# A fused attention and gated-MLP kernel: norm jobs spread over two phases, output weights and splits in other slots

## The chip, the cores and the metric

The kernel runs on one core of a Trainium2 chip. The metric is the device time of one execution in microseconds. Five kinds of work can run beside each other: matrix products on TensorE (PE, with its weight loads PEld), elementwise work on VectorE (DVE), on ScalarE (ACT) and on GpSimd (POOL), and transfers between the chip's memory and its on-chip tiles. All transfers of this kernel are issued from the queue of SyncE (SP). Each engine and SP's queue take their instructions in program order: one that waits holds back all behind it.

## The reference

```python
# u, v: (4, 3008, 256); z: (4, 3008, 64), float32
scores = (z @ z.T) / S                      # S = 3008, for each of the 4 batches
attn = np.maximum(scores, 0.0) ** 2
x = u * (attn @ v)                          # (12032, 256)
rms = np.sqrt(np.mean(x * x, axis=-1, keepdims=True) + 1e-06)
xn = x / rms * rms_g
g = xn @ w_gate                             # w_gate, w_val: (256, 1536), float64
silu = g * (1.0 / (1.0 + np.exp(-g)))
out = (silu * (xn @ w_val)) @ w_out         # w_out: (1536, 256), float64
```

## The kernel before, in words

**Tiling.** The 3008 columns of a batch are cut into six chunks of 512 (the last has 448); two chunks make a *pair* `p`, so there are three pairs in a batch and twelve in all. All products are float32 products on PE, made of a high and a low part: a value is split into `hi` (rounded, made by ACT) and `lo` (the rest, made by DVE or POOL), and each product is three matmuls.

**Phases.** For each pair there is a phase A (attention) and a phase M (the MLP). They run in the order A0, A1, A2, M0, A3, M1, A4, M2 and so on: M lags by three pairs. Phase A has 24 steps, one for each block of 128 rows. A step makes the scores of step i + 2 (4 matmuls, lines 386 and 387, from `mh`, `ml` and `zst`), splits those of step i + 1 (ACT: relu at line 394, `H`; DVE: the square at line 401 and the low half `L` at line 426; in A0 to A2 half of the squares are made by ACT) and multiplies those of step i with `v` (12 matmuls, lines 465, 466 and 470). At its end `emit_gate` multiplies with `u` on DVE and stores `xg`. Where a score's transposed block is needed later, `emit_l` stores a copy (`kept`, from the tile `halves` in the ring `out`), and `load_turned` reads it back in place of a product.

Phase M has twelve *units* of 128 hidden columns. A unit does seven products with combined weights (A11, A12, S1, S2, S3, A22, S4: a Strassen-like scheme on 2 x 2 blocks; lines 664 to 666, from the splits `xh`, `xl` of the pair and the weights `wu`, read by `load_unit` two or three units ahead) and twelve matmuls with the output weights `woh`, `wol` (lines 692, 693 and 696).

**Jobs in slots.** All other work is cut into jobs that `at(phase, slot, fn)` puts into slots: 24 in an A phase (one a step), 36 in an M phase (three a unit). `hook` runs a slot's jobs where the phase's own code calls it, so a job stands in each engine's queue between the phase's own instructions. The jobs that matter here:

- *Norm of a pair* (`norm_jobs`, planned by `norm_plan`): 23 jobs, numbered 0 to 22. Jobs 0 to 7 square the two halves of `ux` on ACT and sum them on DVE, 8 is a small product on PE, 9 to 12 (`guess`, `cubic`, two `newton`) make the reciprocal root on 32 columns, 13 to 18 turn it back and scale `ux` (two transposes, four multiplications of 512 columns), 19 to 22 are four subtractions of 512 columns that make S1, S2, S3 and A22.
- *Splits of a pair* (`split_jobs`, `plan_splits`): seven values, for each a high half on ACT and, a slot later, a low half on DVE.
- *Weights' parts*: the float64 weights come as pairs of 32-bit words (tile `wraw`, in the ring `T` that `wu` and the read-back blocks share) and are decoded by five operations on DVE. `prep_wout(f)` makes the output weights of units f and f + 1 (two operations on ACT and eight pieces on POOL besides: lines 186 and 187). `prep_proj(j)` makes the projections' weights for four units: four parts, then nine `ends` in which `put` writes a high half (ACT), a low half (POOL, four pieces by `pool_pieces`) and two stores to `wcomb`.
- *Batch loads* (`plan_batch`): six chunks of `z` and twelve of `v` of the next batch, each a load, a high half on ACT and a low half on DVE (`z`) or POOL (`v`). Their loads go through a ring of six buffers (`new_raw("batch")`: `mh0`, `ml0`, `mh1`, `ml1` and two of `raw`), which turns by one with each load that is called.

**Order.** `Beside.put` plans M phases: each slot has room for 0.75 us on DVE, every third slot 1.35 on ACT; a job goes into the first slot from its due time on that has room, or, where none has, into the one with the most room left. In A phases the slots are written out by hand. A number `g` from 0 to 71 counts the steps of A0, A1 and A2 together (`at_step`).

## Time and profile before

| | us |
|---|---|
| median of three runs | 2084.29 |
| lowest and highest | 2083.55 and 2086.81 |
| the profiled execution | 2084.4 |
| its span, first to last instruction | 2082.6 |
| PE busy in it | 2030.4 (97%) |
| DVE busy | 1595.1 (77%) |
| ACT busy | 1447.3 (69%) |
| POOL busy | 210.0 (10%) |
| mean granted clock of TensorE | 0.992 |

The span is what the trace covers; the rest of the execution's time lies before the first and behind the last instruction. A granted clock of 1.00 is 2.4 GHz, 0.50 is 1.2 GHz. PE's share is high throughout, so what a change can win or lose lies in the stretches in which PE waits or runs at the lower clock. POOL works mostly in the first fifth of the span, where the weights are decoded; after that it works only for batch loads.

### The profile page before, as it was taken

How to read it: one execution, taken by the hardware profiler on the slowest of the kernel's cores; microseconds unless marked ns; L12 is line 12 of the kernel's file. 1: busy time of each engine (PE TensorE's matmuls, PEld its weight loads, DVE VectorE, ACT ScalarE, POOL GpSimd, SP SyncE). 2: the span in 40 equal slices, each digit the busy share in tenths (PEclk: the TensorE clock that was granted, in tenths of full speed). 3: DMA queues.
4: the chain of work that ended last, by engine and by line, in shares of the span. 5: the costliest groups of instructions: out<-in, count | busy, mean ns of one | idle time of the engine just before them, and what ended most of it. 6: DMA issues, size and time to landing. Idle time of an engine off the chain costs nothing.

```text
span 2082.6 us, 27214 instructions
## 1 busy us (share of the span) xinstructions
PE 2030.4 (97%) x8968; PEld 1680.4 (81%) x8968; DVE 1595.1 (77%) x2633; ACT 1447.3 (69%) x2601; POOL 210.0 (10%) x376
## 2 busy tenths in 40 slices
PE   8998997899999999999999999999999999999999
PEld 7786876688888888888887888788888888888887
DVE  7888886887777777787876776879777687677765
ACT  8887865696577575787577565669756857466665
POOL 0155634200000000500000000130000000000000
PEclk9999998999999999999999999999999999999999
DMA  3244374155456487426355549634645636734342
GB/s 108 79 131 149 109 255 155 72 186 185 129 134 210 135 173 225 162 102 217 135 149 151 183 130 202 214 113 159 206 132 126 207 126 167 193 124 163 124 145 90
DMA packets 320654, 320.50 MB, mean 154 GB/s; under 512 B 196736, under 2 KB 235776, under 8 KB 320512
## 3 DMA queue, kind: packets, MB, share of 16 engines
q1 hardware_dynamic: 320512, 318.77, 50.5%
q8 instruction: 70, 1.15, 0.2%
q14 instruction: 72, 0.59, 0.1%
HBM read 190.78 MB, written 81.79 MB: 131 GB/s over the span
## 4 chain that ended last, share of the span: by engine, by line
PE 75%; DVE 3%; ACT 2%; DMA 1%; issue 1%; SPq 0%; ACTq 0%; DVEq 0%
PE ps L664 9%; PE ps L665 9%; PE ps L666 9%; PE po L465 9%; PE po L466 9%; PE po L470 8%; PE py L692 5%; PE py L693 5%; PE py L696 5%; PE ps L387 3%; PE ps L386 3%; ACT hH L676 1%; DMA raw<-in_zT 1%; DMA out_T<-y 1%; ACT s L671 1%
## 5 line engine op out<-in xcount | busy, mean ns | idle before, releaser
L465 PE MATMUL po<-H,vh 128*128 128x512 f32 (+1 forms) x1152 | 448.3, 389 | 7.6 <-DVE H L430 4.5
L466 PE MATMUL po<-H,vl 128*128 128x512 f32 (+1 forms) x1152 | 445.0, 386 | 0.0
L671 ACT COPY s<-ps 128x512 f32<-128x512 f32 (+1 forms) x432 | 249.8, 578 | 235.5 <-PE ps L666 235.4
L664 PE MATMUL ps<-xh,wu 128*128 128x512 f32 (+1 forms) x1008 | 393.5, 390 | 15.9 <-DMA wu<-wc 11.4
L665 PE MATMUL ps<-xh,wu 128*128 128x512 f32 (+1 forms) x1008 | 389.9, 387 | 2.0 <-DMA wu<-wc 2.0
L666 PE MATMUL ps<-xl,wu 128*128 128x512 f32 (+1 forms) x1008 | 389.3, 386 | 0.0
L470 PE MATMUL po<-L,vh 128*128 128x512 f32 (+1 forms) x1104 | 337.0, 386 | 2.6 <-DVE L L426 2.3
L676 ACT CAST hH<-s 128x512 fp32r<-128x512 f32 (+1 forms) x288 | 176.7, 614 | 202.8 <-DVE s L758 199.2
L426 DVE TENSOR_TENSOR L<-r,H 128x512 fp32r<-128x512 f32 x368 | 255.4, 706 | 52.8 <-ACT H L423 29.6
L401 DVE TENSOR_TENSOR r<-ps,r 128x512 f32<-128x512 f32 x328 | 214.6, 681 | 101.1 <-ACT r L394 100.6
L394 ACT ACTIVATE r<-ps 128x512 f32<-128x512 f32 (+1 forms) x392 | 216.2, 599 | 105.1 <-PE ps L387 93.3
L681 DVE TENSOR_TENSOR hL<-s,hH 128x512 fp32r<-128x512 f32 (+1 forms) x288 | 200.2, 695 | 105.4 <-ACT hH L676 92.3
L465 PEld LDWEIGHTS po<-H,vh 128*128 128x128 f32 x1152 | 216.5, 188 | 59.1 <-DVE H L430 10.4
L466 PEld LDWEIGHTS po<-H,vl 128*128 128x128 f32 x1152 | 216.7, 188 | 40.6
L470 PEld LDWEIGHTS po<-L,vh 128*128 128x128 f32 x1104 | 206.7, 188 | 44.6 <-DVE L L426 5.8
L664 PEld LDWEIGHTS ps<-xh,wu 128*128 128x128 f32 x1008 | 189.6, 188 | 63.0 <-ACT s L671 13.0
L692 PE MATMUL py<-hH,woh 128*128 128x512 f32 (+1 forms) x576 | 223.0, 387 | 8.1 <-ACT hH L676 8.0
L693 PE MATMUL py<-hH,wol 128*128 128x512 f32 (+1 forms) x576 | 222.5, 386 | 0.0
L665 PEld LDWEIGHTS ps<-xh,wu 128*128 128x128 f32 x1008 | 189.8, 188 | 37.6 <-DMA wu<-wc 3.1
L666 PEld LDWEIGHTS ps<-xl,wu 128*128 128x128 f32 x1008 | 189.6, 188 | 36.2
L423 ACT CAST H<-r 128x512 fp32r<-128x512 f32 x328 | 202.7, 628 | 1.2 <-DVE r L401 1.2
L696 PE MATMUL py<-hL,woh 128*128 128x512 f32 (+1 forms) x576 | 175.8, 386 | 0.0
(82 smaller groups left out, 2807.3 us busy)
## 6 DMA issues: line engine op xcount, KB each, us to landing
wu<-wc SPq DMA_DIRECT2D x288, 448.0 KB, 4.0
kept<-halves SPq DMA_DIRECT2D x168, 256.0 KB, 2.0
raw<-in_v SPq DMA_DIRECT2D x44, 256.0 KB, 4.2
u<-in_uT SPq DMA_DIRECT2D x40, 256.0 KB, 4.4
xg<-u SPq DMA_DIRECT2D x40, 256.0 KB, 2.1
raw<-in_zT SPq DMA_DIRECT2D x38, 256.0 KB, 4.9
ux<-xg SPq DMA_DIRECT2D x16, 512.0 KB, 4.9
out_T<-y SPq DMA_DIRECT2D x32, 256.0 KB, 2.2
```

Of the source, the lines that this page charges most:

```text
L394: nc.scalar.activation(a[:, :n], ps[:, :n], AF.Relu)
L426: nc.vector.tensor_tensor(lo[:, :n], a[:, :n], f32(hi[:, :n]), op=ALU.subtract)
L465: nc.tensor.matmul(po[d][:, :n], wh[:, j, ds], hi[:, :n], start=(i == 0), stop=False)
L466: nc.tensor.matmul(po[d][:, :n], wl[:, j, ds], hi[:, :n], start=False, stop=(ends and lo is None))
L470: nc.tensor.matmul(po[d][:, :n], wh[:, j, ds], lo[:, :n], start=False, stop=ends)
L664: nc.tensor.matmul(ps[:, :n], wh[:, o, :], xh[:, :n], start=start, stop=False, skip_group_check=True)
L665: nc.tensor.matmul(ps[:, :n], wl[:, o, :], xh[:, :n], start=False, stop=False, skip_group_check=True)
L666: nc.tensor.matmul(ps[:, :n], wh[:, o, :], xl[:, :n], start=False, stop=stop, skip_group_check=True)
L671: nc.scalar.copy(s, ps[:, :self.n])
L692: nc.tensor.matmul(acc[h, d][:, :n], woh[:, f, ds], hi[:, :n], start=(f == 0), stop=False)
L693: nc.tensor.matmul(acc[h, d][:, :n], wol[:, f, ds], hi[:, :n], start=False, stop=False)
L696: nc.tensor.matmul(acc[h, d][:, :n], woh[:, f, ds], lo[:, :n], start=False, stop=(f == NF - 1))
```

## The change

The ten last norm jobs of pair 0 move from A1 to A2's slots 2 to 11, and its first thirteen stand one in a slot from slot 5 on. Of pair 1's norm the first thirteen stay in M0 (due from slot 3), the last ten go to A3's slots 1 to 10; its splits move from A3's slots 0 to 6 to its slots 16 to 22. Pair 0's splits keep their slots but take another order, with A11 and A12 last. The output weights f = 4 and f = 6 move from M0 to A2, f = 0 and f = 2 three steps earlier, f = 8 and f = 10 get slots 9 and 15 of M0. Batch loads that reuse a buffer are put one slot later. The stores of the weights' parts, and of the kept copies of batch 0, are put on a list that the next hook empties first. The parts' halves use three pairs of tiles that the splits use later (`xh2`, `xl2`, `xh3`, `xl3`, `xh6`, `xl6`) in place of the ring `out`, and the third projection's decoded parts use the tiles of the first. Pair 2's `x` is loaded at M1's start, and its norm is due from slot 4.

```diff
--- before.py
+++ after.py
@@ -98,7 +98,15 @@
     def at(phase, slot, fn):
         jobs[phase, slot].append(fn)
 
+    late = []
+
+    def flush_late():
+
+        while late:
+            late.pop(0)()
+
     def hook(phase, slot):
+        flush_late()
         turns = [t for t in [fn() for fn in jobs.pop((phase, slot), ())] if t]
         while turns:
             for t in list(turns):
@@ -188,6 +196,8 @@
 
         return load, ops + [("a", 0.61, 0, high), ("d", 0.0, 0, low)]
 
+    outs = [2, 3, 6]
+
     def prep_proj(j, pool, tags):
 
         js = slice(j * CH, (j + 1) * CH)
@@ -206,18 +216,23 @@
             parts.append((load, ops + [("d", 0.0, 0, total)]))
 
         def put(o, value):
-            def high():
-                hi = work.tile([P, CH], F32R, tag="out", name="wohi", bufs=3)
-                lo = work.tile([P, CH], F32R, tag="out", name="wolo", bufs=3)
+            def both():
+                outs.append(outs.pop(0))
+                hi = moving.tile([P, CH], F32R, tag=f"xh{outs[-1]}", name="wohi")
+                lo = moving.tile([P, CH], F32R, tag=f"xl{outs[-1]}", name="wolo")
                 x = value()
                 nc.scalar.copy(hi, x)
                 pool_pieces(lo, x, f32(hi), ALU.subtract)
-                for h, t in enumerate((hi, lo)):
-                    nc.sync.dma_start(
-                        out=wcomb[j][:, :, h, o, :].rearrange("f p c -> p f c"),
-                        in_=f32(t).rearrange("p (f c) -> p f c", c=P),
-                    )
-            return high
+
+                def store():
+                    for h, t in enumerate((hi, lo)):
+                        nc.sync.dma_start(
+                            out=wcomb[j][:, :, h, o, :].rearrange("f p c -> p f c"),
+                            in_=f32(t).rearrange("p (f c) -> p f c", c=P),
+                        )
+
+                late.append(store)
+            return both
 
         def combine(key, x, y, op, into=None):
             def go():
@@ -442,9 +457,11 @@
                 else:
                     nc.scalar.copy(halves[:m], split)
                 r0 = 2 * (kt % 4) * P
-                nc.sync.dma_start(
-                    out=kept[b, kc, c][r0:r0 + 2 * m, :].rearrange("(p h) q -> p h q", h=2), in_=halves[:m]
-                )
+                rows = kept[b, kc, c][r0:r0 + 2 * m, :].rearrange("(p h) q -> p h q", h=2)
+                if b == 0:
+                    late.append(lambda rows=rows, part=halves[:m]: nc.sync.dma_start(out=rows, in_=part))
+                else:
+                    nc.sync.dma_start(out=rows, in_=halves[:m])
 
     acc = {}
 
@@ -891,7 +908,10 @@
         at(ph, NK - 1, lambda p=p: load_u(p, [(0, 1), (1, 0), (1, 1)]))
 
     def plan_splits(p, phase, slots):
-        for (one, two), s in zip(split_jobs_at(p), slots):
+        jobs_ = split_jobs_at(p)
+        if p == 0:
+            jobs_ = [jobs_[i] for i in (2, 3, 6, 5, 4, 0, 1)]
+        for (one, two), s in zip(jobs_, slots):
             at(phase, s, one)
             at(phase, s + 1 if s < NK - 1 else s, two)
 
@@ -907,20 +927,20 @@
         done = []
         for k, (load, one, two) in enumerate(todo):
             if k == NC and b == 1:
-                m.put(norm_plan(1), 1)
+                m.put(norm_plan(1)[:13], 3)
             s = max(3 * (k // 2) - 2, 0) + k % 2
             if k >= 6:
-                s = max(s, done[k - 6])
+                s = max(s, done[k - 6] + 1)
             at(m.phase, s, load)
             dve = k < NC
             h = m.put([("a", 0.6, 0, one), ("d", 0.7 if dve else 0.0, 0, two)], s + 2)
             done.append(h if dve else h + 1)
 
 
-    for f, h in zip(range(4, NF, 2), (2, 8, 14, 20)):
+    for f, h in zip(range(8, NF, 2), (9, 15)):
         load, ops = prep_wout(f)
         at(("M", 0), h, load)
-        for k, (e, cost, _, fn) in zip((2, 3, 4, 5, 5, 6, 6, 6), ops):
+        for k, (e, cost, _, fn) in zip((3, 3, 4, 5, 5, 6, 7, 8), ops):
             at(("M", 0), h + k, fn)
             beside[0].room[e, h + k] -= cost if e == "d" else 0.0
 
@@ -930,15 +950,19 @@
 
     at(("A", 1), 3, lambda: load_x(0))
     for i, (e, cost, gap, fn) in enumerate(norm_plan(0)):
-        at(("A", 1), 5 + i * 15 // 23 + (2 if i >= 8 else 0), fn)
+        at(*((("A", 1), 5 + i + (2 if i >= 8 else 0)) if i < 13 else (("A", 2), 2 + i - 13)), fn)
     plan_splits(0, ("A", 2), [16, 17, 18, 19, 20, 21, 22])
     at(("A", 2), NK - 1, lambda: load_x(1))
     for p in range(1, NPAIR):
-        if 1 < p < NPAIR - 1:
+        if p == 2:
+            at(("M", 1), 0, lambda: load_x(2))
+        elif 1 < p < NPAIR - 1:
             at(("A", p + 1), 8, lambda p=p: load_x(p))
         if p < NPAIR - 2:
-            plan_splits(p, ("A", p + 2), range(NO))
+            plan_splits(p, ("A", p + 2), range(16, 16 + NO) if p == 1 else range(NO))
         if p == 1:
+            for i, (e, cost, gap, fn) in enumerate(norm_plan(1)[13:]):
+                at(("A", 3), 1 + i, fn)
             continue
         jobs_ = norm_plan(p)
         m = beside[p - 1]
@@ -948,6 +972,8 @@
             for i, (e, cost, gap, fn) in enumerate(jobs_[:early]):
                 at(("A", p + 1), 12 + i * 8 // early + (2 if i >= 8 else 0) + (1 if i >= 9 else 0), fn)
             jobs_ = jobs_[early:]
+        elif p == 2:
+            start = 4
         elif p == NPAIR - 1:
             at(m.phase, 0, lambda p=p: load_x(p))
             start = 3
@@ -988,7 +1014,7 @@
         at(("A", 0), s, first["v", g][2])
 
 
-    tags_w = [[f"x{h}{k}" for k in ks for h in "hl"] for ks in ((0, 1), (4, 5), (2, 3))]
+    tags_w = [[f"x{h}{k}" for k in ks for h in "hl"] for ks in ((0, 1), (4, 5), (0, 1))]
 
     def at_step(g, fn):
         at(("A", g // NK), g % NK, fn)
@@ -1006,7 +1032,7 @@
         for k, fns in zip((0, 1, 2, 3, 5, 7, 8, 10, 12), ends):
             for fn in fns:
                 at_step(end + k, fn)
-    for f, g in zip(range(0, 4, 2), (57, 61)):
+    for f, g in zip(range(0, 8, 2), (54, 58, 62, 66)):
         plan_part(prep_wout(f), g)
 
     with tc.manual_schedule():
```

## Rows read from the trace of the kernel before

**Rows 1.** The page, part 1: busy us, share of the span, instructions.

```profile
PE 2030.4 (97%) x8968; PEld 1680.4 (81%) x8968; DVE 1595.1 (77%) x2633; ACT 1447.3 (69%) x2601; POOL 210.0 (10%) x376
```

**Rows 2.** Windows of A1, A2, M0, A3, M1 and A2's end: busy us per engine.

```profile
93.35:191.07 97.72, 88.60 (x378) 70.09 (x378) 86.85 (x139) 77.48 (x142) 54.89 (x88) 0.99 0.42 128
191.07:276.96 85.89, 84.15 (x373) 70.60 (x373) 70.84 (x109) 71.37 (x134) 50.68 (x88) 0.97 0.48 137
276.96:402.40 125.44, 103.65 (x429) 82.91 (x429) 95.72 (x158) 74.13 (x136) 44.08 (x80) 0.90 0.49 170
402.40:478.90 76.50, 76.50 (x339) 63.36 (x338) 65.90 (x107) 68.18 (x114) 0.00 (x0) 1.00 0.53 176
478.90:577.41 98.51, 98.34 (x434) 80.78 (x433) 75.11 (x129) 59.37 (x108) 0.00 (x0) 1.00 0.48 145
249.00:273.00 24.00, 24.00 (x113) 20.77 (x112) 23.73 (x36) 19.26 (x39) 22.51 (x34) 1.00 0.40 104
```

**Rows 3.** Timeline of PE at A1's start and end: start, us, [idle before <- releaser].

```profile
93.35 0.50 PE L386 MATMUL ps<-mh,zst 128*128 128x512 f32 x1 [1.32 <-DVE mh L275]
101.77 0.47 PE L465 MATMUL po<-H,vh 128*128 128x512 f32 x1 [1.13 <-DVE u L495]
...
186.35 0.73 PE L470 MATMUL po<-L,vh 128*128 128x512 f32 x2 [1.77 <-DVE L L426]
191.07 0.80 PE L386 MATMUL ps<-mh,zst 128*128 128x512 f32 x1 [3.99 <-DVE mh L275]
201.91 0.47 PE L465 MATMUL po<-H,vh 128*128 128x512 f32 x1 [1.62 <-DVE u L495]
```

**Rows 4.** Timeline of PE in M0.

```profile
343.30 0.80 PE L664 MATMUL ps<-xh,wu 128*128 128x512 f32 x1 [11.06 <-DMA wu<-wc]
...
395.59 0.79 PE L692 MATMUL py<-hH,woh 128*128 128x512 f32 x1 [8.00 <-ACT hH L676]
```

**Rows 5.** Windows behind two gaps: five engines' busy us, then PEclk.

```profile
188.60:195.40 6.80, 4.33 (x9) 3.01 (x10) 5.29 (x9) 1.76 (x3) 3.54 (x9) 0.50 0.46 106
335.40:349.10 13.70, 5.00 (x11) 3.63 (x12) 1.56 (x3) 1.12 (x2) 3.83 (x10) 0.50 0.64 229
```

**Rows 6.** Timeline of SP's queue in M0.

```profile
322.80 16.91 SPq L314 DMA_DIRECT2D raw<-in_v  x2
339.75 0.93 SPq L648 DMA_DIRECT2D wu<-wc  x2
```

**Rows 7.** Timeline of POOL in M0.

```profile
324.39 4.77 POOL L333 TENSOR_TENSOR vl<-raw,vh 128x128 fp32r<-128x128 f32 x8 [2.93 <-ACT vh L322]
...
335.96 3.35 POOL L333 TENSOR_TENSOR vl<-raw,vh 128x128 fp32r<-128x128 f32 x8
```

**Rows 8.** Timeline of DVE at M0's end.

```profile
383.87 0.19 DVE L546 TENSOR_SCALAR misc<-ps 128x32 f32<-128x32 f32 x1
```

**Rows 9.** Timeline of ACT, at A1's end and at M0's end.

```profile
190.17 0.62 ACT L213 CAST wohi<-w 128x512 fp32r<-128x512 f32 x1 [3.31 <-POOL wolo L125]
...
394.92 0.62 ACT L676 CAST hH<-s 128x512 fp32r<-128x512 f32 x1 [10.87 <-DVE s L758]
```

**Rows 10.** Window in A1 of the instructions on tile ux.

```profile
160.00:187.40 27.40, 6.51 (x8) 0.00 (x0) 1.00 0.39 113
```

**Rows 11.** Window at M0's end, DVE alone: busy, PEclk, DMA.

```profile
387.50:394.25 6.75, 6.63 (x11) 0.68 0.01 1
```

**Rows 12.** Window in A2 of the instructions on tile wraw: DVE, ACT, POOL.

```profile
235.00:259.00 24.00, 7.11 (x10) 2.64 (x4) 4.57 (x8) 1.00 0.42 108
```

**Rows 13.** Groups of DVE by line in A2: busy, mean ns | idle before, releaser.

```profile
L426 DVE TENSOR_TENSOR L<-r,H 128x512 fp32r<-128x512 f32 (+1 forms) x42 | 30.6, 751 | 6.7 <-ACT r L421 6.4
```

**Rows 14.** Groups of DVE by line in A3.

```profile
L426 DVE TENSOR_TENSOR L<-r,H 128x512 fp32r<-128x512 f32 x40 | 27.2, 685 | 3.8 <-ACT H L423 3.8
```

**Rows 15.** Timeline of DVE at A1's start.

```profile
98.63 0.69 DVE L401 TENSOR_TENSOR r<-ps,r 128x512 f32<-128x512 f32 x1 [2.69 <-ACT r L394]
```

**Rows 16.** The page, part 6: issues by tile, KB each, median us to landing.

```profile
wu<-wc SPq DMA_DIRECT2D x288, 448.0 KB, 4.0
```

## The prediction

> **What bounds the kernel now.** The page's line of engines comes first: PE is busy for 2030 of 2082.6 us [rows 1], so only time in which PE waits can be won. Next the stretches by stage: A3 and M1 run with PE full, M1 in 98.51 us, while M0, which has the same products, takes 125.44, and A1 has PE busy for only 88.60 of 97.72 [rows 2]. Then PE's own order of time, to see what each gap waits for. At A1's end it waits for DVE: 1.77 us for a low half, 3.99 for `mh`, 1.62 for the gate [rows 3]. In M0 it waits 11.06 us for the weights of unit 7 and 8.00 for ACT's `hH` [rows 4]. After each long gap the granted clock is 0.50, 1.2 GHz of 2.4, for 6.8 and 13.7 us [rows 5], so a long gap costs more than itself.
>
> Each of the two gaps of M0 has one cause. The weights were issued at 339.75, behind a load of `raw<-in_v` that held SP's queue for 16.91 us [rows 6]; it left 0.4 us after POOL's eight pieces of `vl` that began at 335.96 for 3.35 [rows 7]. The code says why: buffers are handed out in the order of the load calls, v-load 6 is called in slot 16, load 5 only in slot 21, so load 6 got the buffer of load 4, which POOL frees after slot 21, behind the low half of an output weight. The second gap is a burst on DVE: from 383.87 on fifteen norm jobs of pair 1 run in one piece [rows 8]; ACT idles 10.87 us for a DVE result behind them [rows 9]. Worked through by hand, the planner put all fifteen into slot 35, because four output weights and the norm filled every slot before.
>
> **The change, part by part.** *A1 loses ten norm jobs of pair 0.* Jobs 13 to 22 go to A2's slots 2 to 11. In A1, beside POOL, eight of them (with `ux`) take 6.51 us and the two transposes, as an estimate, 0.7 each like the rest: 7.9 [rows 10]; in M0, with POOL idle, the whole piece is 6.63 [rows 11]. PE idles 9.12 us in A1 [rows 2]. What stays is what the way from A0 to A1 shows, with less DVE work: 1.32 for `mh`, 1.13 for the gate [rows 3]. So 9.1 - 2.5 = 6.6 can go. The 7.9 us of relief cover it, and they leave slots 12 to 21, where the jobs met the weights' parts. I take -6; bounds -4 (part of the lag is POOL's) and -9 (97.72 to A1's 380 matmuls at M1's rate, 98.51 / 434 = 0.227 us, and those 2.5).
>
> *A2 gains work on DVE*: those ten jobs, and the two output weights f=4 and f=6 out of M0. The two weights that A2 has now cost 7.11 us of DVE and 2.64 of ACT, and POOL 4.57 for the one whose eight pieces fall into the window [rows 12]. So DVE gets 7.1 + 7.2 = 14.3 us. The parts on POOL make DVE slower: a low half takes 751 ns in A2 [rows 13] and 685 in A3, where POOL is idle [rows 14]. POOL is busy for 50.7 of A2's 85.9 us [rows 2]; 9 us more (16 pieces) would add a sixth of that 66 ns to some 110 operations, 1.3 us. DVE is busy 70.84 us in A2; with this 86.4. Of its 15 us of idle time I let 5 remain: 2.69 for ACT at the entry, as in A1's [rows 15], and as an estimate 2 more where ACT's squares and kept copies lead. 86.4 + 5 = 91.4 against 85.89: DVE becomes A2's limit, and A2 grows by 5.5; I take +5. Bounds: all hidden in the idle time, A2 falls to its 372 matmuls (half of them with 448 of 512 columns, 79 us at that rate) and an entry, 82 us, -4; nothing hidden, 14.3 + 1.3 on the path, +15.6. The nearest row is A2's own end: from 249 to 273 us DVE is busy 23.73 us of 24 and PE just keeps up [rows 2], so the added work of slots 14 to 20 has no cover there.
>
> On POOL's price the Trainium skill, SBUF — State Buffer, section "Who interferes with whom", is harsher: DVE with two SBUF inputs and POOL reading SBUF exclude each other for a whole instruction. The means of the two stages agree in sign, not in size. By that rule, as an estimate, each of the 16 pieces (0.42 us unhindered, 3.35 / 8 [rows 7]) could hold DVE for its length, 6.7 us in place of 1.3, and the forecast would be 5.4 us later.
>
> *M0 is emptied.* It loses two output weights (7 us of DVE, 16 POOL pieces) and the norm's last ten jobs. By hand the planner now puts jobs 0 to 12 into slots 14 to 32, none in a burst; the last, `newton`, in slot 32. The burst goes, so the 8.00 us and the slow clock behind it go. v-load 6 still comes ahead of load 5 (slots 16 and 17), but its buffer is that of the last `z` chunk, split by DVE in slot 16, so SP waits for DVE for at most a slot (a third of a unit, 2.5 us). Loads 7 and 8 in slot 20 wait for POOL: eight pieces of an output weight (slot 17), then eight of v (slot 18). Eight pieces take 4.77 or 3.35 us [rows 7], so SP is held some 2 us in slot 20, and the weights of unit 8, then issued, have a unit (33 matmuls, 7.5 us) to land, which takes 4.0 [rows 16]: covered, by 1 to 2 us. I take M1's rate: 98.5 - 125.4 = -27. Bounds: -28, and -20 if unit 8's weights come 4 us late and the clock falls once for some 7 us.
>
> *Stores a step later, three pairs of tiles.* The stores of weights' parts leave SP after POOL has finished, so SP isn't held by them; the `out` ring is no longer shared. The nearest row is ACT's 3.31 us at 190.17, a part's high half kept waiting at A1's end [rows 9]. That lies inside A1's gap, already counted. What is late next: the splits of pair 0 use the tiles 2, 3 and 6 of the last parts, in A2's slots 18 to 20, and the store that frees tile 6 is due in slot 19. It waits for POOL, which is busy 22.51 of the 24 us there [rows 2] and has the low half of f=4 ahead. If POOL is a slot late, ACT stands in slot 20 until the store has landed, up to 2.5 us, with PE's `H` behind it. Bounds 0 and +2.5; I take +1, since the steps get longer and POOL catches up. The four kept stores of pair 2, also a step later, are read back over ten slots on: 0.
>
> *Split order.* M0's first product needs A11, now split in slot 21, A12 in slot 22: their low halves follow DVE's last work of A2, so A2's lag lands on M0's first product; this is in the 91.4.
>
> *A3* takes ten norm jobs (7 us) in slots 1 to 10 where seven splits (4.8 us) were; these go to slots 16 to 22. DVE is busy for 65.9 of 76.5 us there, so the 7 fit: 0 to +2; I take +0.5. Pair 2's norm starts three slots later in M1, which has DVE idle for 23 us: 0. *Moved transfers*: the loads of f=4 and f=6 (512 KB each) go past SP's queue in A2's slots 11 and 15, those of f=0 and f=2 three slots earlier, pair 2's `x` from A3's slot 8 to M1's start, each into a buffer free by then and five or more microseconds ahead of its use: 0.
>
> Sum: -6 + 5 - 27 + 1 + 0.5 = -26.5. The profiled execution took 2084.4 us (2082.6 of span, 1.8 around it), 0.1 from the median of 2084.29, so the forecast is 2058.
>
> **Rivals.** (a) *A2 is hit harder.* DVE's new work finds only some 4 us of idle time to fill: 14.3 + 1.3 - 4 is +12 in place of +5, 2065. For it: POOL and DVE are both nearly full in slots 12 to 20. Against it: DVE's idle time there is mostly waiting for ACT, which a job ahead in the queue fills. The exclusion that the Trainium skill states in the section named above would lead the same way, to 2063 by the estimate there; the two stages' means speak for less, and I give it 0.04 of (a)'s chance. (b) *SP stays the limit of M0.* The buffers still turn in the order of the calls; if POOL is one piece of eight later, unit 8's weights are late by some 4 us, and the clock adds 3: 2065. For it: a margin of 1 to 2 us; against: before, the hold was five slots, now it is under two. (c) *The change does not undo the hold*: the buffer that load 6 gets is again one that POOL frees late. Then the 11 us stay, and some 4 for the matmuls in the slow stretch behind them, 15 in all: 2073. Against it: two `raw` buffers are free of v by then. (d) *A2's work is hidden*: DVE's idle 15 us take all, -4 in place of +5: 2049. (e) *Slower*: in A2 PE now stops a little in every step, and the clock falls and stays at 1.2 GHz. Each matmul then takes twice its 0.227 us or a little less; A2 has 372, so up to +84 and 2142 if it held throughout; it turns the sign from 117 matmuls on. Against it: at A1's end the gap of 1.77 us left the clock at full, it fell behind the 3.99.
>
> **How the numbers follow.** Forecast (2052 to 2062) 0.58, (a) 0.15, (b) 0.12, (c) 0.04, (d) 0.08, (e) 0.03. Range: from 2047, (d) with A1 near its best, to 2069, above (a) and (b); it leaves out (c), (e) and their neighbours. A fifth of a per cent, 4.2 us, is about what can be told from no change here. All but (e) and a rest are faster by more: 0.96; same 0.02, slower 0.02 (from part of (e)).
>
> **What would show it.** M0's window near 98 us with clock 1.00, no wait of PE for `wu` over 1 us, norm jobs of pair 1 spread over M0's last units and A3. A1 near 91 us, its wait for `mh` some 1.3. A2 some 91 us, DVE busy over 85, PE waiting for `L` in gaps under 1 us. A2 under 86 would say (d); SP held by `raw<-in_v` for over 5 us (b) or (c); a stretch of 0.50 in A2 (e). The forecast is wrong if M0 keeps more than 5 us of stalls, or A2 grows by more than 10.

## The result, and the profile after

The changed kernel takes 2066.89 us (median of four runs, 2066.28 to 2068.19) against 2083.92 of the kernel before (2083.48 to 2086.81): a ratio of 0.9918, with an interval of 0.9902 to 0.9934, or 17.0 us less. The forecast was 2058. The sign and the place of the win are the forecast's, the size is nine microseconds short of it. The range of 2047 to 2069 holds the time; the forecast's own 2052 to 2062 does not.

First the page's line of engines of the changed kernel, which answers to [rows 1], then the windows of A1, A2, M0, A3 and M1 in the same order as [rows 2], and two stretches of A1's end and of A2 (columns as there: PE, PEld, DVE, ACT, POOL busy, then PE's clock).

```profile
PE 2028.0 (98%) x8968; PEld 1679.2 (81%) x8968; DVE 1598.0 (77%) x2633; ACT 1448.5 (70%) x2601; POOL 217.3 (11%) x376
```

```profile
93.37:187.66 94.29, 88.59 (x379) 71.51 (x379) 78.90 (x129) 77.25 (x142) 51.81 (x87) 0.98 0.44 132
187.66:280.52 92.86, 87.54 (x373) 70.47 (x374) 84.28 (x126) 73.65 (x138) 65.56 (x102) 0.97 0.48 142
280.52:385.44 104.92, 98.85 (x430) 79.54 (x428) 86.25 (x139) 71.50 (x131) 39.17 (x69) 1.00 0.56 186
385.44:461.50 76.06, 76.06 (x337) 62.81 (x336) 70.23 (x115) 67.79 (x114) 0.00 (x0) 1.00 0.49 167
461.50:560.00 98.50, 98.34 (x435) 81.06 (x434) 77.32 (x132) 60.39 (x111) 0.00 (x0) 1.00 0.52 155
...
177.00:189.00 12.00, 8.59 (x35) 6.30 (x33) 11.73 (x19) 8.48 (x16) 10.07 (x14) 0.91 0.46 132
213.00:279.00 66.00, 61.91 (x276) 50.83 (x275) 65.16 (x96) 52.89 (x102) 54.82 (x80) 1.00 0.42 116
```

Against [rows 2]: A1 -3.4 us, A2 +7.0, M0 -20.5, A3 -0.4, M1 0; -17.3 in all. (A3's window before holds two matmuls more than after; cut at the same matmul, A3 is +0.1 and M1 -0.2.) The profiled execution is 16.2 us of span shorter, since behind M1 it was 1.2 us longer (2066.4 - 560.0 against 2082.6 - 577.4). The two last rows show the new bound: DVE is busy for 11.73 of the last 12 us of A1, and for 65.16 of 66 us of A2, so PE gets no more than DVE hands it.

PE's own timeline names the gaps that are left in place of those in [rows 3, 4].

```profile
187.66 0.80 PE L401 MATMUL ps<-mh,zst 128*128 128x512 f32 x1 [3.34 <-DVE mh L290]
...
284.02 0.50 PE L683 MATMUL ps<-xl,wu 128*128 128x512 f32 x1 [2.89 <-DVE xl L647]
...
371.90 0.50 PE L681 MATMUL ps<-xh,wu 128*128 128x512 f32 x1 [2.48 <-DVE s L775]
```

The waits of 11.06 and 8.00 us are gone. Three gaps of 2.5 to 3.3 us remain, all three for DVE: `mh` at A1's end, A11's low half at M0's start, a sum of M0's last units at 371.9. M0's idle time of 6.07 us (104.92 less 98.85) is the last two and 0.7 of small waits.

SP's queue in M0, where [rows 6] had a load that stood for 16.91 us:

```profile
327.22 0.90 SPq L329 DMA_DIRECT2D raw<-in_v  x2
329.08 0.81 SPq L665 DMA_DIRECT2D wu<-wc  x2
336.21 2.70 SPq L329 DMA_DIRECT2D raw<-in_v  x2
338.96 6.06 SPq L665 DMA_DIRECT2D wu<-wc  x4
```

From 322.4, where the last issue ended, to 327.2 SP stands for the `z` chunk's buffer, and from 329.9 to 336.2 for a buffer that POOL frees; unit 8's weights, issued at 338.96, came half a microsecond late: one weight load waited 0.53 us for them.

The wait at 371.9 is seen in DVE's timeline in M0's last units: the small jobs of pair 1's norm, then the split of pair 3's `mh` and `ml`, then the sum (L775) that PE waits for. POOL's row follows.

```profile
365.14 0.18 DVE L563 TENSOR_SCALAR misc<-ps 128x32 f32<-128x32 f32 x1
...
366.47 0.19 DVE L577 SCALAR_TENSOR_TENSOR misc<-misc 128x32 f32<-128x32 f32 x1
...
367.18 0.46 DVE L580 TENSOR_TENSOR misc<-misc 128x32 f32<-128x32 f32 x1
...
369.37 0.38 DVE L584 SCALAR_TENSOR_TENSOR misc<-misc 128x32 f32<-128x32 f32 x1
...
371.17 0.68 DVE L775 TENSOR_TENSOR s<-ps,s 128x512 f32<-128x512 f32 x1
```

```profile
367.14 3.56 POOL L348 TENSOR_TENSOR vl<-raw,vh 128x128 fp32r<-128x128 f32 x8 [3.44 <-ACT vh L337]
```

The norm's jobs 9 to 12 are thirteen instructions on 32 columns (four of their rows are shown). They take from 365.14 to 369.75, less 0.6 for another job between them: 4.0 us, where the planner books four times 0.35.

At A1's end DVE's timeline shows what stands ahead of `mh`: a weights' part of slots 20 to 22 (L166) and the last two low halves of A1.

```profile
183.74 0.95 DVE L166 SCALAR_TENSOR_TENSOR wraw<-w,wraw 128x512 f32<-128x512 f32 x1
...
185.21 1.80 DVE L441 TENSOR_TENSOR L<-r,H 128x512 fp32r<-128x512 f32 x2
186.93 0.67 DVE L290 TENSOR_SCALAR mh<-raw 128x512 fp32r<-128x512 f32 x1
```

### The profile page after: what moved, and what is told of

Read it like the earlier page. It is cut to its first block, busy times and chain, and to the rows that moved or that the text cites. A ratio compares the mean times of both kernels' runs of the same rounds, so it can differ in the third digit from the quotient of the medians.

```text
span 2066.4 us, 27204 instructions
## 1 busy us (share of the span) xinstructions
PE 2028.0 (98%) x8968; PEld 1679.2 (81%) x8968; DVE 1598.0 (77%) x2633; ACT 1448.5 (70%) x2601; POOL 217.3 (11%) x376
## 3 DMA queue, kind: packets, MB, share of 16 engines
q8 instruction: 70, 1.15, 0.2%
## 4 chain that ended last, share of the span: by engine, by line
PE 76%; DVE 2%; ACT 2%; DMA 1%; issue 1%; SPq 0%; ACTq 0%; DVEq 0%
PE ps L681 10%; PE ps L682 9%; PE ps L683 9%; PE po L482 9%; PE po L483 9%; PE po L487 8%; PE py L709 5%; PE py L713 5%; PE py L710 5%; PE ps L402 3%; PE ps L401 3%; DMA raw<-in_zT 1%; ACT s L688 1%; ACT hH L693 1%; DMA out_T<-y 0%
## 5 line engine op out<-in xcount | busy, mean ns | idle before, releaser
L487 PE MATMUL po<-L,vh 128*128 128x512 f32 (+1 forms) x1104 | 337.9, 387 | 4.4 <-DVE L L441 4.2
L348 POOL TENSOR_TENSOR vl<-raw,vh 128x128 fp32r<-128x128 f32 x144 | 78.9, 584 | 981.8 <-ACT vh L337 981.8
```

What stands on the lines that cost most here:

```text
L487: nc.tensor.matmul(po[d][:, :n], wh[:, j, ds], lo[:, :n], start=False, stop=ends)
```

## The experiments

Twelve runs followed. Each kernel was timed beside the kernel before on its own chip, so ratios are compared, not times: the changed kernel has 0.9918 in its first timing and 0.9915 (0.9902 to 0.9928) when it ran again. The repeat comes first, since it says how finely one profile can be read.

**The changed kernel again** (no edit).

> The changed kernel itself once more, beside the other two on this chip, to see what its stages and its slow-clock stretches do from one execution to the next. Expected: the windows of A1, A2, M0, A3 and M1 within 1 us of 94.3, 92.9, 104.9, 76.0 and 98.6, and 2066 to 2068. Should the gaps be the same ones and the stretches of clock 0.50 differ, then differences of up to 3 us between single profiles of these kernels come from the clock alone.

M0 of that execution, PE's two waits in it, and two windows behind them:

```profile
281.06:389.78 108.72, 102.73 (x429) 82.70 (x428) 86.13 (x139) 71.30 (x131) 39.12 (x69) 0.95 0.53 179
283.50:290.30 6.80, 5.73 (x14) 4.63 (x15) 2.52 (x4) 1.64 (x3) 1.20 (x2) 0.50 0.81 280
375.70:379.10 3.40, 3.23 (x9) 2.52 (x9) 2.66 (x6) 1.85 (x5) 0.00 (x0) 0.50 0.03 7
```

```profile
284.57 0.80 PE L683 MATMUL ps<-xl,wu 128*128 128x512 f32 x1 [2.88 <-DVE xl L647]
...
374.76 0.50 PE L681 MATMUL ps<-xh,wu 128*128 128x512 f32 x1 [2.47 <-DVE s L775]
```

The gaps are the same to 0.01 us, but here the clock is 0.50 for 6.8 and 3.4 us behind them, where the first execution kept 1.00 throughout M0; PE is busy for 102.73 us in place of 98.85. So M0's length alone differs by 3.8 us between two executions of one program. Behind M1 they differ the other way, 1506.3 us in the first and 1502.9 in this one. In what follows gaps, busy times and ratios decide, and M0's idle time rather than its length.

**Norm of pair 0 back in A1.**

```diff
-        at(*((("A", 1), 5 + i + (2 if i >= 8 else 0)) if i < 13 else (("A", 2), 2 + i - 13)), fn)
+        at(("A", 1), 5 + i * 15 // 23 + (2 if i >= 8 else 0), fn)
```

> The changed kernel with all 23 norm jobs of pair 0 in A1, as in the kernel before; all else as changed. Theory (DVE sets A2's length: in the changed kernel it is busy for 5.8 to 6.0 of every 6 us from 213 to 279): A1 goes back from 94.3 to about 97.5 us (+3.3), A2 loses 7.1 us of DVE work and falls from 92.9 to about 87.5 (-5.4), M0 stays near 104.9 or gains up to 1; sum -2 to -3 on 2066.9, about 2064.5. Rival (A2's length comes from the weights' parts on POOL in slots 10 to 20, the ten jobs in slots 2 to 11 ran in idle time): A2 falls by under 2 us, A1 grows by 3.3, the time is about 2069.

Ratio 0.9911 (0.9890 to 0.9932), the changed kernel's own. Its windows of A1 and A2:

```profile
93.23:190.83 97.60, 88.60 (x379) 70.10 (x379) 86.82 (x139) 77.32 (x142) 55.23 (x88) 0.99 0.42 128
190.83:278.71 87.88, 85.12 (x372) 70.78 (x373) 75.66 (x116) 73.41 (x138) 60.10 (x100) 0.97 0.51 153
```

A1 +3.3 and A2 -5.0, where the theory had +3.3 and -5.4. By these windows the ten jobs cost in A2 what they cost in A1, or more; by the ratio, spreading this norm has won nothing that can be told. M0 had 6.8 and 3.4 us of slow clock in this execution, as in the second one of the changed kernel, so its 108.04 us say nothing new.

**One of the two output weights back in M0.** Putting back both was not tried on the chip.

```diff
-    for f, h in zip(range(8, NF, 2), (9, 15)):
+    for f, h in zip(range(6, NF, 2), (3, 9, 15)):
...
-    for f, g in zip(range(0, 8, 2), (54, 58, 62, 66)):
+    for f, g in zip(range(0, 6, 2), (54, 58, 62)):
```

> The changed kernel with the output weight f=6 put back into M0 (slots 3 to 11, 3.6 us of DVE, 8 POOL pieces); f=4 stays in A2. Theory (DVE is A2's limit, and work in A2's slots 18 to 20 has no cover; M0 has some 12 us of idle DVE at 98.5): A2 and the wait at M0's first product together lose 3.6 us plus 0.5 for POOL, M0 else grows by 0 to 2 since pair 1's norm jobs come later by two slots; about 2064. Rival (M0 is what the weights fill: the norm jobs gather in its last slots again as they did before, where they made PE wait 8.0 us): M0's window goes to 110 or more, the time is about 2070.

Ratio 0.9929 (0.9910 to 0.9947): A2 -1.6 us, M0 109.32, A3 +1.3. M0's length and the time (2069 by the ratio) are nearly the rival's, its reason is not. SP's queue and, last, ACT's and PE's rows in M0:

```profile
326.93 0.88 SPq L665 DMA_DIRECT2D wu<-wc  x2
337.92 1.41 SPq L329 DMA_DIRECT2D raw<-in_v  x3
```

```profile
340.43 0.62 ACT L337 CAST vh<-raw 128x512 fp32r<-128x512 f32 x1 [6.90 <-DMA raw<-in_v]
```

```profile
342.11 0.79 PE L681 MATMUL ps<-xh,wu 128*128 128x512 f32 x1 [5.40 <-ACT s L688]
```

One weight more, and a load of `v` stands on SP from 327.8 to 337.9; ACT's split of that chunk waits 6.90 us for it, and the copies of the products behind it make PE wait 5.40, with 0.50 of clock for 6.8 us from 340.8 on. The hold is that of the kernel before and of the prediction's rival (b), a load that stands for a buffer which POOL frees; its way to PE is another, through ACT's queue and not through late weights. So with one weight back SP is no longer free. In the total time this weight is worth 2 to 3 us by the ratios, no more than their intervals leave open.

**Norm of pair 1 whole in M0.**

```diff
-                m.put(norm_plan(1)[:13], 3)
+                m.put(norm_plan(1), 3)
...
-            for i, (e, cost, gap, fn) in enumerate(norm_plan(1)[13:]):
-                at(("A", 3), 1 + i, fn)
```

> The changed kernel with all 23 norm jobs of pair 1 planned into M0, the last ten taken out of A3; the splits of pair 1 stay in A3's slots 16 to 22. Theory (even with two output weights gone, the jobs in M0 leave no room: by the planner's costs the last ten land in slots 32 to 35): a burst of about 7 us stands before M0's last copies and A3's entry; M0 goes from 104.9 to some 112, with a stretch of 0.50, A3 keeps 76; about 2074. Rival (the burst was the four weights' doing alone, and its gain in the change came from the weights moved): M0 stays within 1 us of 104.9, A3 within 0.5 of 76.1; about 2067.

Ratio 0.9944 (0.9924 to 0.9964), 5 to 6 us worse than changed. M0's window, and the gap that came back:

```profile
280.71:391.66 110.95, 101.41 (x430) 81.61 (x428) 93.14 (x149) 71.51 (x132) 39.89 (x69) 0.97 0.53 177
```

```profile
385.60 0.80 PE L709 MATMUL py<-hH,woh 128*128 128x512 f32 x1 [3.50 <-ACT hH L693]
```

The theory, though its burst is half the old one: `hH` is late again, by 3.50 us where it was 8.00; DVE is busy for 93.1 us of M0, against 95.7 in the kernel before [rows 2]. A3 keeps 76.0 us with or without the ten jobs: they really are free there.

**Another order of pair 0's splits.**

```diff
-            jobs_ = [jobs_[i] for i in (2, 3, 6, 5, 4, 0, 1)]
+            jobs_ = [jobs_[i] for i in (0, 2, 1, 3, 4, 5, 6)]
```

> The changed kernel with the splits of pair 0 in another order (A11, S1, A12, S2, S3, A22, S4 in A2's slots 16 to 22), so that A11's low half is out five slots before M0's first product. Theory (the 2.9 us at M0's start wait for A11's low half alone, which stands last in DVE's queue): the wait goes, M0's window falls from 104.9 to about 102, A2 as before; about 2064. Rival (DVE is late by that much as a whole, so that PE next waits for the last L of A2 instead): the wait moves by one instruction, A2 and M0 together fall by under 0.7 us; about 2066.5. A loss is possible too: if a tile of the last parts is not free when A12 or S3 is split, ACT waits for it in slots 18 to 20 and A2 grows by 1 to 2.

Ratio 0.9900 (0.9883 to 0.9916), 3 to 4 us better than changed, which the intervals leave open; windows A2 94.11, M0 103.23. PE no longer waits at M0's start at all, but in A2:

```profile
266.26 0.50 PE L482 MATMUL po<-H,vh 128*128 128x512 f32 x1 [1.52 <-ACT H L438]
```

The wait for A11's low half is gone (M0 has 3.39 us of idle time for 6.07), and 1.3 us of it came back in A2, where ACT stood 3.23 us for a tile that POOL had not yet left (a difference of two weights, read out of the tile that A11 takes). The loss that the expectation allowed for took half of the gain.

**Two weights' parts earlier in A1.**

```diff
-(2, (40, 44, 48, 51), 54)
+(2, (39, 42, 48, 51), 54)
```

> The changed kernel with two of the last weights' parts of A1 earlier: their DVE work in slots 15 to 17 and 18 to 20 in place of 16 to 18 and 20 to 22. Theory (the 3.7 us at A1's end, and the clock of 0.50 for 6.8 us behind it, come from the part in slots 20 to 22, which stands in DVE's queue ahead of mh; DVE has 5.8 us or more of work in every 6 from 171 to 189, but is idle for 2.1 of 6 around 162): PE's wait for mh falls to under 2 us, the clock stays at full; A1 falls from 94.3 to some 91.5, A2 by up to 1.7; M0 as before; about 2063. Rival (DVE is short of time as a whole from A1's second half to A2's end, where it is busy for 5.8 to 6.0 of every 6 us): what A1's end wins comes back as waits for L in A2 or at M0's start; the sum of A1, A2 and M0 stays within 1 us of 292.1.

Ratio 0.9918 (0.9900 to 0.9935), as changed. PE at A1's end:

```profile
177.28 0.74 PE L487 MATMUL po<-L,vh 128*128 128x512 f32 x2 [0.72 <-DVE L L441]
...
186.99 0.80 PE L401 MATMUL ps<-mh,zst 128*128 128x512 f32 x1 [2.28 <-DVE mh L290]
```

The wait for `mh` shrinks by 1.1 us, a new one for L stands at 177, A1 is 0.5 us shorter, A2 0.2 longer: the rival. (M0's 108.46 us hold 102.69 of busy time at a mean clock of 0.95, so the sum of the three windows says nothing here.) The part in slots 20 to 22 is not the cause by itself; DVE has too much work from there on.

**Small norm jobs of pair 1 into A3.**

```diff
-                m.put(norm_plan(1)[:13], 3)
+                m.put(norm_plan(1)[:8], 3)
...
-            for i, (e, cost, gap, fn) in enumerate(norm_plan(1)[13:]):
+            for i, (e, cost, gap, fn) in enumerate(norm_plan(1)[8:]):
```

> The changed kernel with five more norm jobs of pair 1 (the folding matmul and the four jobs on small columns behind it) out of M0's last units, into A3's slots 1 to 5; the ten after them in slots 6 to 15. Theory (PE's wait of 2.9 us at 369 in M0 is for a copy of DVE behind these small jobs, planned at 0.35 us each, 1.4 in all, but taking 4.5 us from 365 to 370): the wait goes, M0 falls from 104.9 to about 102, A3, with DVE busy 70 of 76 us, takes the 4.5 us as 0 to +2; about 2065. Rival (the mh and ml of pair 3 in the same slots make the wait): M0 stays within 0.7 us of 104.9, A3 grows by up to 2; about 2068.

Ratio 0.9898 (0.9881 to 0.9915). M0:

```profile
281.30:386.10 104.80, 100.64 (x428) 81.54 (x426) 83.02 (x126) 71.35 (x131) 40.02 (x69) 0.97 0.56 186
```

The wait at 371.9 is gone and no other takes its place: M0's idle time falls from 6.07 to 4.16 us (a wait of PE of 0.84 us for unit 8's weights shows in it now), A3 grows by 0.2 to 76.3. M0's length stays, since this execution had 6.8 us of slow clock at its start. So the small jobs made that wait.

**Without the POOL pieces of f=4 and f=6.** Their units take the low parts of the four weights before them.

```diff
+            if f in (4, 6):
+                return
             wh, wl = tiles["wh"], tiles["wl"]
...
-                nc.tensor.matmul(acc[h, d][:, :n], wol[:, f, ds], hi[:, :n], start=False, stop=False)
+                nc.tensor.matmul(acc[h, d][:, :n], wol[:, f - 4 if 4 <= f < 8 else f, ds], hi[:, :n], start=False, stop=False)
```

> The changed kernel without the 16 low pieces on POOL of the output weights f=4 and f=6 in A2 (their units take the low parts of the four weights before them, so part of the computation is another one); PE, ACT and DVE have the same work. Theory (the pieces slow DVE by what the means of two stages showed, 1.3 us in all): A2 and the wait at M0's start together fall by 1 to 2 us, DVE's mean for a low half in A2 by under 3%; about 2065.5. Rival (while a piece runs, a DVE instruction of two inputs stands still for the length of the piece, as the Trainium skill states in SBUF - State Buffer, Who interferes with whom; by the 0.42 us of a piece as an estimate 6.7 us): A2 and M0's start together fall by 6 us or more, since DVE is the limit there; about 2061.

Ratio 0.9902 (0.9887 to 0.9917). A2 is 91.71 us, 1.15 less, and the wait at M0's start 1.66 in place of 2.89:

```profile
281.81 0.50 PE L685 MATMUL ps<-xl,wu 128*128 128x512 f32 x1 [1.66 <-DVE xl L649]
```

Together 2.4 us for 16 pieces: nearer to the 1.3 of the two stages' means than to 6.7. (The changed kernel's A2 took 92.86 and 93.15 us in its two executions, the wait 2.89 and 2.88, so 2.4 is clear of what one execution does.) DVE by line in A2, each shape by itself, first of the changed kernel, with its A3, and then without the pieces (busy, mean ns):

```profile
L441 DVE TENSOR_TENSOR L<-r,H 128x512 fp32r<-128x512 f32 x22 | 16.6, 756 | 0.0
L416 DVE TENSOR_TENSOR r<-ps,r 128x512 f32<-128x512 f32 x16 | 10.9, 679 | 0.0
...
L441 DVE TENSOR_TENSOR L<-r,H 128x512 fp32r<-128x512 f32 x40 | 27.2, 684 | 3.3 <-ACT H L438 3.2
L416 DVE TENSOR_TENSOR r<-ps,r 128x512 f32<-128x512 f32 x41 | 26.5, 682 | 2.5 <-ACT r L409 2.2
```

```profile
L443 DVE TENSOR_TENSOR L<-r,H 128x512 fp32r<-128x512 f32 x22 | 16.4, 745 | 0.0
```

A low half of 512 columns, with both inputs in SBUF, takes 756 ns in A2 and 684 in A3, where POOL is idle (those of 448 columns, which only A2 has, 802); the product `r<-ps,r`, with one input in PSUM, takes 679 and 682. Here the Trainium skill, SBUF — State Buffer, section "Who interferes with whom", agrees: a DVE instruction with two SBUF inputs contends with a POOL instruction that reads SBUF. Its exclusive lock, taken for the whole length of each piece, would have made the 16 pieces cost up to 6.7 us by the estimate in the prediction; the runs show 2.4.

**Stores at once, in the old ring.**

```diff
-                outs.append(outs.pop(0))
-                hi = moving.tile([P, CH], F32R, tag=f"xh{outs[-1]}", name="wohi")
-                lo = moving.tile([P, CH], F32R, tag=f"xl{outs[-1]}", name="wolo")
+                hi = work.tile([P, CH], F32R, tag="out", name="wohi", bufs=3)
+                lo = work.tile([P, CH], F32R, tag="out", name="wolo", bufs=3)
...
-                late.append(store)
+                store()
```

> The changed kernel with the stores of the weights' parts issued at once again and their halves in the three buffers of the ring that the kept copies use too, as in the kernel before. Theory (these two edits of the change are worth little by themselves, since the waits they concern lie beside a full DVE): A1, A2 and M0 together within 2 us of 292.1; 2066 to 2069. Rival (they carry much of the win: the old ring makes ACT wait for a store's landing in each of the parts' last steps, as it did for 3.31 us at 190 in the kernel before, and SP, held by the stores, issues loads late): A2 or A1 grow by 4 us or more, and a stretch of clock 0.50 more; over 2071.

Ratio 0.9915 (0.9900 to 0.9930); A1, A2 and M0 are 94.05, 93.05 and 105.02, together 292.1 as changed. Late stores of the parts and the three pairs of tiles are worth nothing that can be told here.

**More squares of A2 on ACT.**

```diff
-        return p < LAG and (i + k) % 2 == 1 and not is_turned(p, i, k) and (p < LAG - 1 or i < NK - 8)
+        return p < LAG and (i + k) % 2 == 1 and not is_turned(p, i, k) and (p < LAG - 1 or i < NK)
```

> The changed kernel with every second square of A2's last eight steps on ACT instead of DVE, as in its other steps: eight products of 0.65 us, some 5 us, leave DVE, ACT gets eight squares of 0.55 us. Theory (DVE is what sets A2's length from 213 us on; ACT is busy for 4.4 to 5.3 of every 6 us there and has the room): A2 and the wait at M0's first product together lose 3 to 5 us, L's waits in A2's second half shrink; some 2063. Rival (the weights' parts on POOL and ACT set the end of A2, and ACT comes late with H when it is given more): A2 within 1 us of 92.9 or longer, PE waits for H in place of L; 2067 or more.

Ratio 0.9914 (0.9900 to 0.9928), as changed. In the changed kernel, as before, DVE makes all squares of A2's last eight steps, so this moves work off it where it is fullest. A2 is 92.04 us, 0.8 less. PE at M0's start:

```profile
279.99 0.50 PE L682 MATMUL ps<-xh,wu 128*128 128x512 f32 x1 [1.06 <-DMA wu<-wc]
281.36 0.58 PE L683 MATMUL ps<-xl,wu 128*128 128x512 f32 x1 [0.88 <-DVE xl L647]
```

Neither expectation: DVE did become earlier, but PE then waits for the weights of M0's unit 0, not for ACT's `H`. A second limit lies right behind DVE.

**Combined**: the squares and the small norm jobs as above, and `mh` of pairs 1 and 2 on ACT.

```diff
-            nc.vector.tensor_scalar(mh[:, :n], tiles["raw"][:, :n], SCALE, None, op0=ALU.mult)
+            if p in (1, 2):
+                nc.scalar.activation(mh[:, :n], tiles["raw"][:, :n], AF.Copy, scale=SCALE)
+            else:
+                nc.vector.tensor_scalar(mh[:, :n], tiles["raw"][:, :n], SCALE, None, op0=ALU.mult)
```

> Three edits at once on the changed kernel: the squares of A2's last steps on ACT (as in the run beside it), the folding matmul and four jobs on small columns of pair 1 in A3 instead of M0's last units (tried alone before, where the wait of 2.9 us at 369 went), and mh of the pairs 1 and 2 made by ACT, so that at A1's and A0's end only ml stands behind DVE's queue. Theory (three places at which DVE is late, each for itself): A1 -1 to -2, A2 with M0's start -3 to -5, M0's end -2.5; 2058 to 2061. Rival (the waits hang together, since DVE or then ACT is late as a whole: relief at one place shows as a wait at the next): no better than the better of its parts, 2063 to 2066.

2059.24 us, ratio 0.9883 (0.9869 to 0.9897), on the chip on which the changed kernel had 2064.59: 5.3 us better and inside the theory's 2058 to 2061. Its terms did not come out one by one: A1 is 90.14 us, A2 93.61, M0 101.28. A1's window ends at A2's first matmul, which needs `mh` alone; PE's wait for `ml`, 2.41 us, now stands behind that matmul and counts in A2. SP's queue shows the second limit:

```profile
271.61 0.36 SPq L229 DMA_DIRECT2D wc<-wolo  x1
272.06 0.96 SPq L668 DMA_DIRECT2D wu<-wc  x2
```

Unit 0's weights are read at 272.06, behind the store of the last part, which stood on SP until POOL had made it at 271.6, behind eight pieces of an output weight (262.8 to 268.8).

**Parts first**: the combined kernel with the weights' work in another order.

```diff
-(2, (40, 44, 48, 51), 54)
+(2, (40, 43, 47, 50), 53)
...
-    for f, g in zip(range(0, 8, 2), (54, 58, 62, 66)):
+    for f, g in zip(range(0, 8, 2), (55, 59, 63, 67)):
...
-            jobs_ = [jobs_[i] for i in (2, 3, 6, 5, 4, 0, 1)]
+            jobs_ = [jobs_[i] for i in (2, 3, 0, 1, 4, 5, 6)]
```

> The combined kernel with the order of A1's and A2's last weights' work changed: three of the last four weights' parts and what follows them one slot earlier, the four output weights one slot later (so that two of them, not three, have their POOL pieces ahead of the last part's), and A11 and A12 split in A2's slots 18 and 19. In the combined kernel M0 waits first for the weights of its unit 0 (1.1 and 1.0 us), which are read back behind the store of the last part, whose low half POOL ends at 271.6, behind eight pieces of an output weight; then for A11's low half (1.6 us). Theory (POOL's order, not its load, makes the first wait, and the split's place the second): M0's three waits of 3.7 us in all fall under 1, A1's end waits less for ml (2.9 us, with a part one slot earlier); some 2055. Rival (DVE is late as a whole and the output weights' decoding is now nearer to the end): PE waits for L or xl in A2's last steps instead, the sum of A1, A2 and M0 stays within 1.5 us of the combined kernel's 285.0; 2059.

2051.17 us (2050.40 to 2052.12), ratio 0.9846 (0.9832 to 0.9859): the fastest of all, some 32 us ahead of the kernel before. A1, A2 and M0, and SP's queue:

```profile
92.34:182.72 90.38, 87.18 (x379) 70.30 (x379) 76.36 (x125) 77.25 (x143) 49.09 (x84) 1.00 0.44 138
182.72:273.28 90.56, 85.37 (x374) 70.11 (x374) 81.91 (x121) 77.41 (x145) 68.05 (x101) 0.98 0.51 153
273.28:372.00 98.72, 97.22 (x427) 79.62 (x426) 83.43 (x127) 71.84 (x133) 41.85 (x71) 1.00 0.57 194
```

```profile
264.47 0.36 SPq L229 DMA_DIRECT2D wc<-wolo  x1
264.92 0.93 SPq L668 DMA_DIRECT2D wu<-wc  x2
```

Unit 0's weights leave 7.1 us earlier, M0 starts without a wait and reaches M1's rate, the 98.5 of the forecast. POOL's busy time in A2 is nearly that of the combined kernel (68.05 us, 69.27 there): the order made that wait, not the load. At A1's end PE still waits 2.64 us for `ml`: that part of the expectation failed, as it did when two parts were moved alone. A1, A2 and M0 together are 279.7 us, 5.4 less than in the combined kernel (285.0). Its profiled execution was 6.3 us shorter behind M1 too (1501.7 against 1507.9), where no edit reaches; so of the nearly eight us by the ratio the windows show 5.4.

## Why the prediction was right, and where its sizes were off

**The mechanism held.** Both of M0's long waits went. With the whole norm back the burst's wait returns (3.50 us). With one weight back SP's hold returns (10.1 us, 327.8 to 337.9) and costs PE a wait of 5.40, though through ACT and not through late weights. The batch loads put a slot later bear on the same hold and were undone in no run, so how the relief divides between them and the weights is not shown. M0 won 20.5 us, more than the whole result. A2 paid for it, as forecast, and DVE is A2's limit: 65.16 busy of 66 us. A3 took the ten jobs for nothing (76.03 against 75.93, cut at the same matmul; forecast +0.5), and the moved transfers cost nothing that a row shows.

**M0's term was mis-sized: -20.5, not -27.** Two steps failed. The first is "A2's lag lands on M0's first product; this is in the 91.4". It was not: A2 used up 92.86 us by itself, and 2.89 more at M0's start came on top, with A11's low half last in DVE's queue. Ordering the splits otherwise removed that wait, but alone gave half of it back to A2. The second is "the planner now puts jobs 0 to 12 into slots 14 to 32, none in a burst": the slots are what the planner's code gives, but I took its 0.35 us for each small job, 1.4 in all, where they take 4.0 (some 1.2 of it because six of the thirteen instructions took twice as long beside POOL) and make PE wait 2.48. Taking them out removed that wait. These two are 5.4 of the 6.5 us; the rest is 0.7 us of small waits and 0.4 of busy time beyond M1's 98.5. Unit 8's weights, whose margin of 1 to 2 us was used up, are a part of the small waits only.

**A1's term was mis-sized: -3.4, not -6**, below its bound of -4. PE's idle time in A1 fell from 9.12 to 5.70 us, where the sum let 2.5 stay. The step is "what stays is what the way from A0 to A1 shows": 1.32 us for `mh`. 3.34 stayed, with 6.8 us of slow clock behind it, because DVE is full at A1's end even without the ten jobs (11.73 of 12 us). Neither moving the parts by one to two slots nor taking `mh` off DVE removed it; the second turned it into a wait for `ml` (2.41).

**A2's term: +7.0, forecast +5 and +1 for the stores.** DVE is busy for 84.28 us, against 86.4 in the sum, and idle for 8.6, not 5: of the 15 us that it had idle its new work filled 6.5, where the forecast let it fill 10 and rival (a) 4. With the 2.89 at M0's start A2's work cost 9.9 us, so rival (a), +12 and 2065, described A2 better than the forecast did, and by its first reason, the idle time; POOL's 16 pieces, its other ground, cost 2.4 us in all. The prediction's price for POOL rested on two means of unlike shapes: the 751 ns of [rows 13] mix 777 for 512 columns with 720 for 448, so like with like the difference to 685 is 92 ns, not 66. The stores' term of +1 is not to be seen in the run with the old ring (292.1 us for the three stages in both).

**What the sum hid.** That -6 for A1 and half of the +5 for A2 are one edit. Undone alone it gives 3.3 us to A1 and takes 5.0 from A2, with the same total time: the norm of pair 0 won nothing that can be told. What is left for the win is the two output weights, pair 1's norm and the later batch loads. Undone one by one, a weight is worth 2 to 3 us by the ratios and the norm 5 to 6, well under the 17 together. By how much each alone would have helped is open, since both weights back in M0 was not tried.

**The other rivals.** (b) stands one weight away: SP was held by loads of `v` for 4.8 and 6.3 us, the second beyond the 5 that I had named as its sign, yet unit 8's weights came only half a microsecond late in this execution. (c), (d) and (e) are excluded by the rows: the 11 us for `wu` are gone, A2 did not fall, and its clock stayed at 1.00 from 213 to 279 us (a stretch of 0.50 stands at its entry, behind the wait for `mh`, as before the change). Of the two signs that the prediction set against itself one came true: M0 kept 6.07 us of stalls, over 5; A2 grew by 7.0, under 10. By that sign the forecast failed in M0. The range holds the time because it was drawn to take in rivals (a) and (b), not because the forecast's terms came out.

## What to carry to other kernels

When work moves from a stage with idle time on PE to one before it, book the lag at the end of that stage as a term of its own: it lands on the next stage's first product. Price small instructions by count and by their own rows (0.18 to 0.46 us each here), not by a planner's cost for the job. And where two engines are full together, look for the order as well as the load: here the same work in another order was worth nearly eight microseconds more by the ratio, 5.4 of them in the stages concerned, where taking squares off DVE by itself was worth nothing that could be told.

## What was not expected of the hardware

The granted clock is not the same behind the same gap: behind 2.89 us at M0's start it stayed at 1.00 in one execution, and behind 2.88 it was 0.50 for 6.8 us in another of the same program, which with a second stretch of 3.4 us cost M0 3.9 us of busy time.

An instruction of 128x32 on DVE took 0.18 to 0.19 us with POOL idle, and mostly 0.34 to 0.46 beside POOL. In the changed kernel the change comes at 367.18, 0.04 us after POOL had begun its pieces of `vl`. The kernel before shows the other end: POOL's pieces run from 384.12 to 385.85, the instruction that starts at 385.50 takes 0.40, the next one 0.19. And in the run with these jobs in A3, where POOL is idle, all thirteen take 0.18 to 0.19. DVE and POOL before, then DVE in that run:

```profile
385.50 0.40 DVE L558 TENSOR_TENSOR misc<-misc 128x32 f32<-128x32 f32 x1
385.93 0.19 DVE L560 SCALAR_TENSOR_TENSOR misc<-misc 128x32 f32<-128x32 f32 x1
```

```profile
384.12 1.73 POOL L333 TENSOR_TENSOR vl<-raw,vh 128x128 fp32r<-128x128 f32 x4 [3.72 <-ACT vh L322]
```

```profile
404.77 0.18 DVE L580 TENSOR_TENSOR misc<-misc 128x32 f32<-128x32 f32 x1
```

So beside POOL the smallest instructions doubled, while the low halves of 512 columns grew by a tenth (684 to 756 ns). Two inputs in SBUF seem not to be needed for it: the `TENSOR_SCALAR` at 385.10 in the kernel before, with one, took 0.37 us (one row).
